# A chain of attention, routed experts and an FFT mixer: narrow experts reordered, one decode moved ahead

## The chip, the cores and the metric

The kernel runs on one core of one Trainium2 chip. The time is the device time of one execution in microseconds; the figure for a kernel is the median of its runs.

## What is computed

Three stages follow each other: attention with a local window and global keys, a stage of routed experts, and a mixer with a two-dimensional FFT. The change lies in the second:

```python
B, S, D, E, F = 2, 768, 512, 8, 1024
logits = x @ w_gate                     # one expert per token
local = sigmoid(x @ w_local)
for each sequence, for each token s:
    e = argmax(logits[s]) if s == 0 or local[s] < 0.5 else the expert of token s - 1
    out[s] = softmax(logits[s])[e] * (relu(x[s] @ w1[e]) @ w2[e])
```

The mixer behind it adds the real part of the FFT over tokens and features, normalises, and applies two dense layers (`w_ch1`, 512 x 2048, and `w_ch2`) with a residual. All data are float32.

## The kernel before

**Matrix products in two parts.** A float32 value is split in a high part that TensorE takes in one pass (`hi`) and the rest (`lo`). ScalarE (ACT) casts the high part, VectorE (DVE) subtracts it from the value. A product is then hi x hi, hi x lo and lo x hi: three matmuls for each step of the contraction. Weights, rows and hidden values all pass through this pair of steps.

**The ring of weights** (`Ring`). An expert has four pieces of 1 MB, kind `"e"`: two of w1, two of w2. A piece is loaded by SP into one of four raw buffers (`load`) and split into a slot (`take`: L1048 the cast on ACT, L1050 the subtract on DVE, in two halves of 1024 columns); when its last half is done, SP loads the piece that stands four places later into the buffer. The order of all pieces is the list `seq`. Between the experts' pieces stand eight of kind `"d"`: weights of the mixer that come as 64-bit words and are decoded to float32 ahead of time, so that the mixer can load them plain. A decode is one step on ACT (`start`, L1081), four on DVE (`bits`, L1090, L1092, L1094, L1096), all on a tile `dec` from a pool of two, and a DMA on POOL's queue that writes `dec` to `wmf` (L1014). `shade` says which decodes come with which expert's pieces: before, 2, 1, 1, 2, 1, 1 and 0 for experts 0 to 6.

**An expert** (`Moe.expert`). The tokens were sorted into lists by expert. A block is up to 128 tokens; POOL gathers its rows into a tile xg (`gathers`, L1133), PE turns them (`turn`, L1164), ACT and DVE split them into xh and xl (L1167, L1168). While expert e computes, the background `bg` prepares expert e + 1: its weights (`take`) and the turning of its rows (`tokens`). A call of `step` between matmuls lets the background issue one or more of its steps.

- *Wide* (two blocks): `first256` forms the hidden values of both, 256 columns wide (L1224), with relu by ACT and DVE (L1227, L1228); `third` adds a third block if there is one; `second` (L1204) multiplies by w2, block by block; `write` scales and scatters the result.
- *Narrow* (one block): `first128` forms h with tokens as rows (L1254), in two halves of 512. ACT copies each half out (`hs`, L1259), PE turns it (L1243), ACT and DVE form hh and hl (L1245, L1246). The second product starts when the first half's hh is there.

A branch at run time on the number of blocks chooses wide or narrow, on every engine. Expert 0 is always wide. In the runs here experts 1, 2, 3 and 5 are wide and experts 4 and 6 are narrow. Expert 7 is worked by sequence, two blocks with `first128`, and a third block with what is left of both; behind the turning of the third stands the check `rest(more)` for tokens beyond it, of which there are none here.

**The order ahead of expert 0** (`run`). The rows of expert 0 have to be gathered, after the list of tokens is written and its entries are loaded. Meanwhile PE multiplies constants (`keep_busy`, L50: 6, 6 and 3 matmuls of 512 columns), POOL and DVE clear the four xg tiles, and POOL issues two gathers and a scatter. The engines get to this place by a jump out of the attention's code.

**What sets the order.** Each engine works through its own instructions in the order in which this code issues them; the background decides between which matmuls a cast or a subtract comes to stand. DMA issues wait in the order of their queue: SP's for weights and entries, POOL's for gathers, scatters and the write to `wmf`.

## Time and profile before

| what | us |
|---|---|
| median of 3 runs (631.21 to 633.63) | 632.18 |
| the profiled execution, its own time | 635.4 |
| its span, first to last instruction | 633.6 |
| PE busy in the span | 609.5 |
| DVE busy | 383.8 |
| ACT busy | 275.3 |
| POOL busy | 100.5 |

The mean granted clock of PE is 0.992 of full speed. On PE the first matmul of expert 0 starts at 127.17 us. A row in order of time gives the start, the duration, engine, line, operation, what it writes and reads, how many like it are run together, and in brackets for how long the engine had been idle before and what ended that; "issue" there means that the profile names nothing. A releaser is inferred from the times of semaphores.

### The profile page before, as it was taken

What the parts mean: (1) busy time and instruction counts of PE and PEld (TensorE: products, weight loads), DVE (VectorE), ACT (ScalarE), POOL (GpSimd) and SP (SyncE); (2) the same over time, 40 slices, a digit from 0 to 9 for tenths busy, and PEclk for the clock granted to TensorE, in tenths of its full rate; (3) what the DMA queues carried; (4) which work ended last, traced back from release to release, by engine and by line L of the source; (5) the groups of instructions that cost most, each with busy time, mean ns of one, the idle gap of its engine ahead of it and who ended that gap; (6) DMA issues with size and microseconds to landing.
All of it is one profiled execution on the core that took longest, in us unless ns stands there. A gap on an engine that the chain in (4) does not pass through costs nothing.

```text
span 633.6 us, 9722 instructions
## 1 busy us (share of the span) xinstructions
PE 609.5 (96%) x3506; PEld 494.1 (78%) x3507; DVE 383.8 (61%) x898; ACT 275.3 (43%) x548; POOL 100.5 (16%) x147
## 2 busy tenths in 40 slices
PE   9999998799999969898999999999999999999997
PEld 4777875499899849687867887888888888888885
DVE  5778786279786968661389987997531221272112
ACT  5789883266475556552434533441121221131010
POOL 2146662315313312300100000000000000000000
PEclk9999999999999989989999999999999999999999
DMA  8568762279978989961260242551100100100001
GB/s 278 187 204 203 201 120 68 49 283 337 372 250 278 335 288 327 339 210 66 87 250 32 95 173 92 187 190 63 67 0 1 32 36 0 67 2 0 1 0 66
DMA packets 25192, 92.49 MB, mean 146 GB/s; under 512 B 7645, under 2 KB 8797, under 8 KB 17185
## 3 DMA queue, kind: packets, MB, share of 16 engines
q1 hardware_dynamic: 19664, 79.50, 37.6%
q0 software_dynamic: 4736, 10.56, 4.6%
q10 hardware_dynamic: 720, 1.55, 0.7%
q8 instruction: 36, 0.59, 0.4%
q14 instruction: 36, 0.29, 0.2%
HBM read 81.00 MB, written 14.84 MB: 151 GB/s over the span
## 4 chain that ended last, share of the span: by engine, by line
PE 52%; DVE 1%; ACT 0%; issue 0%; DVEq 0%; ACTq 0%
PE h L1742 21%; PE acc L1757 7%; PE acc L1756 7%; PE acc L1758 7%; PE y L1204 1%; PE acc L1576 1%; PE acc L1562 1%; PE more L1254 1%; PE h L1254 1%; PE more L1204 1%; PE f L1708 1%; PE f L1605 1%; PE h L50 1%; PE f L1627 0%; DVE u L1767 0%; PE acc L1565 0%
## 5 line engine op out<-in xcount | busy, mean ns | idle before, releaser
L1747 DVE SCALAR_TENSOR_TENSOR hl<-h,hh 128x512 fp32r<-128x512 f32 x48 | 33.1, 689 | 117.5 <-ACT hh L1746 117.5
L1746 ACT ACTIVATE hh<-h 128x512 fp32r<-128x512 f32 x48 | 28.8, 600 | 164.3 <-PE h L1742 164.3
L1050 DVE TENSOR_TENSOR wide<-raws,wide 128x1024 fp32r<-128x1024 f32 (+1 forms) x38 | 44.8, 1201 | 24.4 <-ACT wide L1048 24.4
L168 ACT ACTIVATE t<-t,nm 128x256 f32<-128x256 f32 (+1 forms) x96 | 46.0, 480 | 10.7 <-DVE nm L159 9.9
L1742 PE MATMUL h<-un0h,wide 128*128 128x512 f32 (+1 forms) x136 | 42.4, 378 | 0.1
L1048 ACT CAST wide<-raws 128x1024 fp32r<-128x1024 f32 (+2 forms) x42 | 40.6, 993 | 4.1 <-PE acc L1758 3.4
L159 DVE CUSTOM_DVE_ANT_0 t<-sp,bias 128x256 f32<-128x256 f32 (+1 forms) x96 | 32.8, 398 | 8.3 <-PE sp L150 4.4
L1757 PE MATMUL acc<-wide,hh 128*128 128x512 f32 x96 | 37.8, 393 | 0.0
L1756 PE MATMUL acc<-wide,hh 128*128 128x512 f32 x96 | 37.6, 392 | 0.0
L1758 PE MATMUL acc<-wide,hl 128*128 128x512 f32 x96 | 37.5, 390 | 0.0
L1133 POOL DMA_INDIRECT xg<-xs,ent x23 | 28.7, 1250 | 39.9 <-PE y L1204 17.4
L1742 PEld LDWEIGHTS h<-un0h,wide 128*128 128x128 f32 x136 | 25.0, 188 | 5.0 <-ACT un0h L1517 0.3
L178 PE MATMUL tp<-consts,t 128*128 128x128 f32 x176 | 26.1, 283 | 1.7 <-ACT p L184 1.7
L178 PEld LDWEIGHTS tp<-consts,t 128*128 128x128 f32 x176 | 18.9, 141 | 9.3 <-ACT p L184 4.9
L1742 PE MATMUL h<-un0l,wide 128*128 128x512 f32 (+1 forms) x68 | 25.6, 377 | 0.0
L192 PE MATMUL sm<-p,vs 128*64 128x128 f32 x352 | 24.5, 279 | 0.0
L184 ACT COPY p<-tp 128x512 f32<-128x512 f32 (+1 forms) x48 | 24.3, 537 | 0.3 <-PE tp L178 0.3
L1081 ACT ACTIVATE dec<-raws 128x1024 f32<-128x1024 f32 x18 | 20.6, 1143 | 4.8 <-issue 4.8
L1224 PE MATMUL h<-xh,wide 128*128 128x256 f32 x160 | 22.5, 279 | 0.0
L1096 DVE SCALAR_TENSOR_TENSOR dec<-raws,dec 128x1024 int32<-128x1024 int32 x18 | 22.0, 1225 | 0.6
L1094 DVE SCALAR_TENSOR_TENSOR dec<-raws,dec 128x1024 int32<-128x1024 int32 x18 | 22.0, 1222 | 0.4
L192 PEld LDWEIGHTS sm<-p,vs 128*64 128x64 f32 x352 | 18.7, 136 | 3.8 <-issue 3.8
(474 smaller groups left out, 1602.3 us busy)
## 6 DMA issues: line engine op xcount, KB each, us to landing
raws<-we SPq DMA_DIRECT2D x31, 1024.0 KB
raws<-wm SPq DMA_DIRECT2D x18, 1024.0 KB
raws<-wmf SPq DMA_DIRECT2D x7, 1024.0 KB
wmf<-dec POOLq DMA_DIRECT2D x8, 512.0 KB
xs<-xrow SPq DMA_DIRECT2D x12, 260.0 KB
vs<-v SPq DMA_DIRECT2D x6, 512.0 KB
raws<-kq SPq DMA_DIRECT2D x3, 1024.0 KB
u<-x SPq DMA_DIRECT2D x6, 512.0 KB
```

The lines of the kernel that those rows point to most:

```text
L159: V.tensor_tensor_reduce(out=u.t[:, x, :u.W], in0=u.sp[:, j, k, :u.W], in1=bias[:, 4 * u.g + x, u.b0:u.b0 + u.W], scale=-0.125, scalar=3.0 ...
L168: A.activation(u.t[:, x, :u.W], u.t[:, x, :u.W], AF.Exp, bias=u.nm[:, x:x + 1], scale=-1.0, accum_out=u.den[:, x])
L178: T.transpose(u.tp[k][:, j, c], u.t[:, 2 * k + j, c * P:(c + 1) * P], st.ident)
L192: T.matmul(turned[j * D:j * D + D, k], vs[:, ti % KS, u.h + 2 * k + j], u.p[:, 2 * k + j, c], start=c == 0, stop=c == len(tiles) - 1)
L1048: (first or nc.scalar.copy)(hi[:, cs], raw[:, cs])
L1050: (eng() if callable(eng) else eng or nc.vector).tensor_tensor(lo[:, cs], raw[:, cs], hi[:, cs].bitcast(F32), op=ALU.subtract)
L1742: nc.tensor.matmul(ps[:, c], a[:, k], x[:, k, c], start=n == 0, stop=n == 11)
L1746: nc.scalar.activation(hh, ps, AF.Relu)
L1747: nc.vector.scalar_tensor_tensor(hl, ps, 0.0, hh.bitcast(F32), op0=ALU.max, op1=ALU.subtract)
L1756: T.matmul(acc[c], hh[:, cs], h2, start=first, stop=False)
L1757: T.matmul(acc[c], hh[:, cs], l2, start=False, stop=False)
L1758: T.matmul(acc[c], hl[:, cs], h2, start=False, stop=last)
```

## The change

- Only experts 2, 4 and 6 (the third, fifth and seventh) branch on the number of blocks. Experts 1, 3 and 5 always go the wide way. The hint to PE on the next branch stands at experts 1, 3 and 5.
- The narrow way takes one background step at a time in place of two, first the two pieces of the next expert's w1, then those of w2, then decodes if any. Its `hs` lie in the third rows' tile and a `ys` tile, not in `dec`.
- The decodes are spread 2, 1, 2, 1, 0, 1 and 0 over experts 0 to 6, and one (`FIRST`) comes before expert 0: it is the fifth piece of the ring, and DVE makes its first step, by two shifts, in place of ACT's.
- POOL clears all four xg tiles. Of the fill-in matmuls ahead of expert 0 the middle six are cut in four parts of 128 columns each.
- In expert 7 the third block's rows are turned in the background of the first block, and the check `rest(more)` stands behind the third block's result.

```diff
--- before.py
+++ after.py
@@ -43,11 +43,13 @@
 L2, L3 = 2, 3
 
 
-def keep_busy(nc, st, ps, n):
+def keep_busy(nc, st, ps, n, parts=1):
 
     x = st.busy
-    for _ in range(n):
-        nc.tensor.matmul(ps, x[:, :1].to_broadcast([P, P]), x.unsqueeze(1).to_broadcast([P, 8, D]), start=True, stop=True)
+    w = 8 // parts
+    for k in range(n * parts):
+        o = k % parts * w * D
+        nc.tensor.matmul(ps[:, o:o + w * D] if parts > 1 else ps, x[:, :1].to_broadcast([P, P]), x.unsqueeze(1).to_broadcast([P, w, D]), start=True, stop=True)
 
 
 def load_kq(nc, st, io, i, pairs=((0, B * H // 2),)):
@@ -671,6 +673,8 @@
 SPLIT = 6
 WARM = 6, 6, 3
 TOKENS = 4
+FIRST = 1
+DECODED = 2, 1, 2, 1, 0, 1, 0
 CASTS = (5, 6, 7, 8)
 RESTS = (24, 25, 26, 27)
 AHEAD = dict(enumerate([0, 1, 2, 2, 2, 1, 1, 1, 4, 0, 0, 0, 0, 0, 1, 0, 0, 4, 1, 1, 1, 0, 0, 0, 2, 1, 1, 1], 4))
@@ -948,7 +952,7 @@
         self.behind, self.whole = [], 2
         self.seq = []
         self.plan = self.shade()
-        self.seq = [("e", g) for g in range(4)]
+        self.seq = [("e", g) for g in range(4)] + [("d", n) for n in range(FIRST)]
         for a, b in self.plan:
             self.seq += a + b
         for m in range(len(MIX)):
@@ -958,14 +962,14 @@
     @staticmethod
     def shade():
 
-        d = iter([("d", n) for n in range(2 * EARLY)])
+        d = iter([("d", n) for n in range(FIRST, 2 * EARLY)])
         plan = []
         for e in range(E - 1):
             g = 4 * e + 4
             a = [("e", g), ("e", g + 1)]
             b = [("e", g + 2), ("e", g + 3)]
 
-            for _ in range(-(-min(e + 1, E - 2) * 2 * EARLY // (E - 2)) + -min(e, E - 2) * 2 * EARLY // (E - 2)):
+            for _ in range(DECODED[e]):
                 (a if len(a) == 2 else b).append(next(d))
             plan.append((a, b))
         plan.append(([("t", 0), ("t", 1)], []))
@@ -1004,7 +1008,7 @@
         r = self.at[kind, n]
         raw = self.st.raw[r % PIECES]
         if kind == "d":
-            words, t = self.start(r)
+            words, t = self.start(r, nc.vector if n < FIRST else None)
             yield
             for k, _ in enumerate(self.bits(words, t)):
                 if k != 0:
@@ -1072,13 +1076,16 @@
         hi, lo, raw = self.quarter(n, k)
         self.tc.nc.vector.tensor_tensor(lo, raw, hi.bitcast(F32), op=ALU.subtract)
 
-    def start(self, r):
+    def start(self, r, by=None):
 
         if r in self.begun or r >= len(self.seq) or self.seq[r][0] not in ("m", "m2", "d") or (self.seq[r][0] != "d" and MIX[self.seq[r][1]][0] < EARLY):
             return self.begun.get(r)
         t = self.work.tile([P, PW // 2], F32, name="dec")
         words = self.st.raw[r % PIECES].bitcast(I32).rearrange("p (n two) -> p n two", two=2)
-        self.tc.nc.scalar.activation(t, words[:, :, 1].bitcast(F32), AF.Abs)
+        if by:
+            by.tensor_scalar(t.bitcast(I32), words[:, :, 1], 1, 1, op0=ALU.logical_shift_left, op1=ALU.logical_shift_right)
+        else:
+            self.tc.nc.scalar.activation(t, words[:, :, 1].bitcast(F32), AF.Abs)
         self.begun[r] = words, t
         return words, t
 
@@ -1126,7 +1133,7 @@
         self.ps_x = pool("ps_x", 2, space=PSUM)
         self.ps_more = pool("ps_more", 3, space=PSUM)
         self.ps_y = pool("ps_y", 1, space=PSUM)
-        for x in self.xg[:2]:
+        for x in self.xg:
             tc.nc.gpsimd.memset(x, 0.0)
 
     def gather(self, out, table, idx):
@@ -1288,12 +1295,13 @@
             self.weight(e, (2,))
 
             with tc.If(n > 2):
-                for _ in self.turn(2, 0, self.place(e, 2)):
-                    pass
+                if e < LAST:
+                    for _ in self.turn(2, 0, self.place(e, 2)):
+                        pass
+                late = self.first128(w1, *self.more, spare, spare)
+                result(2, self.more[1], spare, "more", lambda: None, late)
                 if e == LAST:
                     self.rest(more)
-                late = self.first128(w1, *self.more, spare, spare)
-                result(2, self.more[1], spare, "more", lambda: None, late)
 
         def pieces():
             for units in ring.plan[e]:
@@ -1323,26 +1331,33 @@
                     result(at + 1, own(hs, 1), spare, "more")
 
         def narrow():
-            first, then = pieces()
-            bg.add(chain(*first))
+            units = [u for part in ring.plan[e] for u in part]
+            for u in units:
+                if u[0] == "d":
+                    ring.begun.pop(ring.at[u], None)
+            takes = {u: ring.take(*u) for u in units}
+            d = [takes[u] for u in units if u[0] == "d"]
+            bg.add(chain(*(takes["e", 4 * e + 4 + k] for k in range(2))))
             h = own((self.hh[0], self.hl[0]), 0)
-            late = self.first128(w1, own((self.xh[e % 2], self.xl[e % 2]), 0), h, (self.ps_h, "h"), (self.ps_x, "xtp"), step)
+            late = self.first128(w1, own((self.xh[e % 2], self.xl[e % 2]), 0), h, (self.ps_h, "h"), (self.ps_x, "xtp"), bg.step,
+                                 [self.place(e, 2)[:, :DM], self.work.tile([P, DM], F32, name="ys", bufs=2)])
             bg.drain()
-            bg.add(chain(*then))
+            bg.add(chain(*(takes["e", 4 * e + 6 + k] for k in range(2)), *d))
             calls = iter(range(8))
 
             def behind():
                 if next(calls) == TOKENS:
                     bg.add(self.tokens(e + 1))
-                bg.step(2)
+                bg.step()
 
             result(0, h, (self.ps_y, "y"), "ys", behind, late)
 
         if e < LAST:
             if e + 2 < E:
                 self.entries(e + 2)
+            if e % 2 and e + 1 < LAST:
                 tc.mark_branch_hint_location(f"wide{e + 1}", hint=(ahead > 1), engines=[mybir.EngineType.PE])
-            if e == 0:
+            if e == 0 or e % 2:
                 wide()
                 return
             with tc.If(n > 1, label=f"wide{e}") as arm:
@@ -1351,6 +1366,7 @@
                 narrow()
             return
 
+        bg.add(self.turn(2, 0, self.place(e, 2)))
         for c in range(2):
             x, h = (own(s, c) for s in ((self.xh[e % 2], self.xl[e % 2]), (self.hh[0], self.hl[0])))
             late = self.first128(w1, x, h, (self.ps_h, "h"), (self.ps_x, "xtp"), step, [x[:, :DM] for x in self.xg[:2]])
@@ -1421,24 +1437,25 @@
         nc = tc.nc
         ring = st.ring
         self.entries(0, (1, 2))
-        for x in self.xg[2:]:
-            nc.vector.memset(x, 0.0)
         rows = self.gathers(0, (1, 2))
         self.entries(1)
         w = ring.load(2 * PIECES - 2)
         tc.add_manual_dep(w.ins, rows[1].ins.name, mybir.DependencyInfo(mybir.DependencyClass.Sync, mybir.DependencyReason.DATA),
                           reason="this load would hold the rows up")
         self.scatter(st.ye, st.ent0[:, 1:2])
+        for n in range(FIRST):
+            for _ in ring.take("d", n):
+                pass
         spare = self.ps_more.tile([P, DM], F32, name="more")
         keep_busy(nc, st, spare, WARM[0])
         counts = nc.values_load(st.nch[0:1, E + 1:E + 2], min_val=0, max_val=2 * 4 ** E - 1)
-        keep_busy(nc, st, spare, WARM[1])
+        keep_busy(nc, st, spare, WARM[1], 4)
         for _ in self.tokens(0):
             pass
         keep_busy(nc, st, spare, WARM[2])
         ring.load(2 * PIECES - 1, nc.scalar)
         for e in range(E):
-            self.expert(e, (counts >> 2 * e) & 3 if e < LAST else counts >> 2 * e, counts >> 2 * E, (counts >> 2 * (e + 1)) & 3 if e + 2 < E else None)
+            self.expert(e, (counts >> 2 * e) & 3 if e < LAST else counts >> 2 * e, counts >> 2 * E, (counts >> 2 * (e + 1)) & 3 if e % 2 and e + 1 < LAST else None)
 
 
 def post(tc, ctx, st):
```

**ACT, the narrow way.** `wide` and `sl5h` are slots of the ring, `raws` its raw buffers. ACT in expert 4's narrow code, from the end of expert 3. Before:

```order
L1348 UNCONDITIONAL_BRANCH
L1048 CAST wide<-raws 128x1024 x4
L1259 COPY dec<-h 128x512
L1081 ACTIVATE dec<-raws 128x1024
L1245 ACTIVATE hh_6327<-xtp 128x4x128
L1259 COPY dec<-h 128x512
L1048 CAST wide<-raws 128x1024
L1245 ACTIVATE hh_6327<-xtp 128x4x128
```

The change:

```order
L1363 UNCONDITIONAL_BRANCH
L1052 CAST wide<-raws 128x1024 x2
L1266 COPY xg_6353<-h 128x512
L1052 CAST wide<-raws 128x1024
L1252 ACTIVATE hh_6327<-xtp 128x4x128
L1052 CAST wide<-raws 128x1024
L1266 COPY ys<-h 128x512
L1052 CAST wide<-raws 128x1024
L1252 ACTIVATE hh_6327<-xtp 128x4x128
```

Two casts have moved from ahead of the first copy of h to behind it, one by one, and the decode is gone from between the copy and hh.

**PE, expert 7's third block.** The rows from the second half of the first block to the third. Before:

```order
L1254 MATMUL h<-wide,xl_6349 128x512 x2
L1254 MATMUL h<-sl5h,xl_6349 128x512 x2
L1290 REGISTER_ALU
L1290 COMPARE_AND_BRANCH
L1164 MATMUL more<-consts,xg_6354 128x128 x4
L1395 REGISTER_ALU
L1395 COMPARE_AND_BRANCH
```

The change, from the start of expert 7:

```order
L1363 UNCONDITIONAL_BRANCH
L1261 MATMUL h<-wide,xh_6346 128x512 x3
L1171 MATMUL more<-consts,xg_6354 128x128 x4
L1261 MATMUL h<-wide,xh_6346 128x512
L1261 MATMUL h<-sl5h,xh_6346 128x512
```

and at the end of the first block:

```order
L1261 MATMUL h<-wide,xl_6349 128x512 x2
L1261 MATMUL h<-sl5h,xl_6349 128x512 x2
L1297 REGISTER_ALU
L1297 COMPARE_AND_BRANCH
L1261 MATMUL more<-wide,xh_6347 128x512 x4
```

The four transposes of the third rows (`more<-consts,xg`) have moved ahead by a whole block, and the third block's matmuls follow its branch without the check between.

**DVE, the wait for the first rows.** From the jump out of the attention to the first rows. Before:

```order
L1913 UNCONDITIONAL_BRANCH
L1425 MEMSET xg_6353 128x520
L1425 MEMSET xg_6354 128x520
L1434 TENSOR_LOAD nch
L1168 TENSOR_TENSOR xl_6348<-xtp,xh_6345 128x4x128 x2
```

The change:

```order
L1930 UNCONDITIONAL_BRANCH
L1086 TENSOR_SCALAR dec<-raws 128x1024
L1097 TENSOR_SCALAR dec<-dec 128x1024
L1099 TENSOR_SCALAR dec<-dec 128x1024
L1101 SCALAR_TENSOR_TENSOR dec<-raws,dec 128x1024
L1103 SCALAR_TENSOR_TENSOR dec<-raws,dec 128x1024
L1451 TENSOR_LOAD nch
L1175 TENSOR_TENSOR xl_6348<-xtp,xh_6345 128x4x128 x2
```

Five steps of a decode stand where the two memsets stood, ahead of the load of the block counts and of the first rows' xl.

## Rows read from the trace of the kernel before

**Rows 1.** Windows: busy us of PE, PEld, DVE, ACT, POOL; PEclk, DMA share, GB/s.

```profile
200.00:220.00 20.00, 19.85 (x128) 17.76 (x127) 18.88 (x25) 12.91 (x16) 4.55 (x4) 1.00 0.77 267
220.00:240.00 20.00, 14.54 (x56) 11.15 (x55) 13.44 (x14) 11.55 (x15) 4.19 (x5) 0.83 0.82 292
260.00:280.00 20.00, 17.97 (x78) 14.36 (x78) 10.10 (x10) 10.61 (x14) 5.38 (x5) 0.91 0.78 274
```

**Rows 2.** What PE waited for, 126 to 325 us: total, times, longest.

```profile
PE y L1204 <- ACT hh L1245: 4.3, 1, 4.3
PE h L1254 <- ACT wide L1048: 2.0, 1, 2.0
PE more L1254 <- DVEq L1395: 1.6, 1, 1.6
```

**Rows 3.** PE in order of time, expert 4: start, us, instruction [idle before <-releaser].

```profile
220.58 1.09 PE L1254 MATMUL h<-wide,xh 128*128 128x512 f32 x4
...
226.10 0.66 PE L1243 MATMUL xtp<-consts,dec 128*128 128x128 f32 x4 [1.16 <-ACT dec L1259]
...
232.45 0.79 PE L1204 MATMUL y<-sl0h,hh 128*128 128x512 f32 x1 [4.30 <-ACT hh L1245]
...
242.30 1.10 PE L1224 MATMUL h<-xh,wide 128*128 128x256 f32 x8
```

**Rows 4.** PE in order of time, experts 6 and 7.

```profile
267.92 0.47 PE L1254 MATMUL h<-sl0h,xh 128*128 128x512 f32 x1 [2.03 <-ACT wide L1048]
...
275.56 1.32 PE L1204 MATMUL y<-wide,hh 128*128 128x512 f32 x5
...
282.44 1.10 PE L1254 MATMUL h<-wide,xh 128*128 128x512 f32 x4
...
288.47 0.60 PE L1164 MATMUL more<-consts,xg 128*128 128x128 f32 x4
290.67 1.16 PE L1254 MATMUL more<-wide,xh 128*128 128x512 f32 x4 [1.60 <-DVEq L1395]
```

**Rows 5.** ACT in order of time, expert 4.

```profile
221.66 3.90 ACT L1048 CAST wide<-raws 128x1024 fp32r<-128x1024 f32 x4
225.47 0.58 ACT L1259 COPY dec<-h 128x512 f32<-128x512 f32 x1
230.80 1.12 ACT L1081 ACTIVATE dec<-raws 128x1024 f32<-128x1024 f32 x1 [4.75 <-issue]
```

**Rows 6.** POOL in order of time, the write-out ahead of expert 4's decode.

```profile
221.12 0.59 POOL L1014 DMA_DIRECT2D wmf<-dec  x1 [0.68 <-DVE dec L1096]
```

**Rows 7.** DVE in order of time, expert 4's first subtracts.

```profile
222.80 4.63 DVE L1050 TENSOR_TENSOR wide<-raws,wide 128x1024 fp32r<-128x1024 f32 x4 [1.98 <-ACT wide L1048]
```

**Rows 8.** ACT in order of time, the end of expert 5.

```profile
257.33 2.02 ACT L1048 CAST wide<-raws 128x1024 fp32r<-128x1024 f32 x2
```

**Rows 9.** DVE in order of time, the wait for the first rows.

```profile
120.62 1.04 DVE L1425 MEMSET xg<- 128x520 f32 x2 [4.15 <-issue]
126.60 1.29 DVE L1168 TENSOR_TENSOR xl<-xtp,xh 128x512 fp32r<-128x512 f32 x2 [4.95 <-ACT xh L1167]
```

**Rows 10.** One decode's DVE steps: the window 231.9 to 236.4 us, tile dec alone.

```profile
231.90:236.40 4.50, 3.83 (x4) 0.50 0.45 189
```

**Rows 11.** PE in order of time, the wait for the first rows.

```profile
121.12 2.76 PE L50 MATMUL more<-busy 128*128 128x512 bf16 x12 [1.46 <-issue]
125.20 1.29 PE L1164 MATMUL xtp<-consts,xg 128*128 128x128 f32 x8 [1.31 <-issue]
```

**Rows 12.** POOL in order of time, three gathers.

```profile
121.55 1.02 POOL L1133 DMA_INDIRECT xg<-xs,ent  x1 [0.31 <-issue]
...
147.36 3.10 POOL L1133 DMA_INDIRECT xg<-xs,ent  x1 [3.39 <-PE more L1204]
...
215.44 1.33 POOL L1133 DMA_INDIRECT xg<-xs,ent  x1 [4.35 <-PE y L1204]
```

**Rows 13.** The page's part 2: GB/s in 40 equal slices of the span.

```profile
GB/s 278 187 204 203 201 120 68 49 283 337 372 250 278 335 288 327 339 210 66 87 250 32 95 173 92 187 190 63 67 0 1 32 36 0 67 2 0 1 0 66
```

## The prediction

> **What bounds the kernel now.** I read the profile in this order: windows of 20 us, the list of what TensorE (PE) waited for, then the rows in time order of each engine around the places that those two point to. In the windows the reader is to see that PE works nearly without a gap while wide experts run (19.85 of 20 us), and that two windows fall out: 220 to 240 us, where PE is busy 14.54 of 20 us at a granted clock of 0.83, and 260 to 280, with 17.97 at 0.91 [rows 1]. The waits from the first expert to the tail are few: 4.3 us for hh, 2.0 us at an h, 1.6 us at the third block [rows 2], and 1.16 us for a copy in expert 4 [rows 3]. The branches of the wide experts are not among them. So the time of this stage is PE's, and what can be won is those four waits and the slow clock behind two of them.
>
> **Expert 4** is narrow and lasts from 220.58 to 242.30, 21.72 us [rows 3]. What would it last if PE never waited, at full clock? The same work is seen undisturbed in two pieces: a first product with its four transposes from 282.44 to 288.47, 6.03 us, and a second with its twelve transposes from 275.56 to 282.44, 6.88 us [rows 4]. Together 12.91 us. The difference, 8.81 us, is what the present order costs, and two steps of ScalarE (ACT) make it. First, ACT has four casts ahead of the copy of h (3.90 us from 221.66), so the copy comes at 225.47 and PE's transposes wait 1.16 us [rows 3, 5]. Second, ACT's decode step (L1081) starts only at 230.80, after 4.75 us of idling, and the hh that PE needs stands behind it in ACT's order, so PE waits 4.30 us [rows 3, 5]. The row names no releaser. The step writes a `dec` tile; there are two of these, the narrow way holds its hs in one, and the other's former content was sent to `wmf` by a DMA issued only at 221.12 [rows 6]. So the step waits for that write to end, or for its raw piece. After the wait PE runs slow: 0.83 over 20 us is 6.8 us at the lower of its two clocks, 1.2 GHz. That is the rest of the 8.81 us.
>
> The change takes both away: two casts, not four, stand ahead of the copy, no decode is issued in expert 4 at all, and the hs lie in xg2 and ys. What is late next is VectorE (DVE). It has eight subtracts, 1.16 us each in a row of four, the first at 222.80 behind the first cast, 2.2 us after the expert's start [rows 7]; that takes it to 11.5 us. Two hl and two xl come on top; a pair of xl lasts 1.29 us [rows 9], so 2.6 us more, 14.1 us without any gap. Following the new order by hand, with the gaps where DVE waits for PE, I get the second xl at 14.9. PE has its 12.91 us, then eight matmuls of expert 5 that need only xh, 0.12 us apart, 0.93 us, and so wants that xl at 13.84: a new wait of 0.3 to 1.1 us. I take 1.1. Expert 4 gives 8.81 - 1.1 = **7.7 us**; bounds 6 (one more wait like the 1.6 us) and 8.5.
>
> **Expert 6** is narrow too. PE stops for 2.03 us ahead of its first matmul and then loses clock (0.91 of the window) [rows 1, 4]. From 267.92 to 282.44 are 14.52 us. The work alone is 12.91, so the slow clock costs 1.61 us, and the stop adds 2.03: 3.64 us lost. The wait names an ACT cast, but the last one that this matmul can mean ended at 259.35 [rows 8]. So it is none of the data, and I read it as PE's own instruction stream after the jump into the narrow code. Expert 4 is entered by the same jump, without a stop [rows 3]. What differs is where the code lies: counted in the program, a matmul as two instructions, the narrow code of expert 6 begins 2 instructions ahead of a multiple of 256, that of expert 4 begins 122 ahead. In the changed program the two begin 116 and 98 ahead. The bounds are 0 and 3.6; I take **3.6**, since both new places are like the one that did not stop.
>
> The Trainium skill (Runtime: NRT & Kernel Launch, "Instruction fetch mechanics") says that instructions come in blocks of 256, fetched in order, and that a taken branch out of the window forces a fetch. The stop agrees with it, though no row here tells a fetch from another stall. By that rule alone a taken jump over a whole wide way would stop wherever it lands; expert 6 would then gain nothing and the sum be 8.6 us.
>
> **Expert 7's third block.** PE turns it at 288.47 and then waits 1.60 us, behind the check for rows beyond the third block, which isn't taken, and the xl that DVE makes after it [rows 4]. In the changed order the turn stands behind the third matmul of the first block, some 5 us ahead of its use, and the check behind the third result. The transposes are only moved. **1.6 us**, bounds 1.0 and 1.6.
>
> **The wait for the first rows.** Here the change adds. DVE is idle from 121.66 to 126.60 [rows 9] and now gets a decode in place of two memsets. Four steps of a decode last 3.83 us [rows 10]; the first is new (two shifts on DVE in place of ACT's step), and I bound it by 0.7 us, a short step of those four, and 1.2 us, a long one. From 120.62 the decode ends at 125.1 to 125.7, ahead of the xl at 126.60, so DVE's own time costs nothing; without that cover its 4.5 to 5.1 us would stand ahead of the xl. POOL's two more memsets lie ahead of the list's entries, which its gathers wait for. The 24 short fill-in matmuls have the columns of the six that they replace: PE's twelve took 2.76 us from 121.12, and PE then idled 1.31 us to the transposes at 125.20 [rows 11], so they may grow by 1.3 us for nothing.
>
> What costs is the gathers. The second of this place took 1.02 us beside an idle DVE; beside DVE's subtracts and decodes a gather took 1.33 us, and once 3.10 us [rows 12]. For two gathers that bounds the cost at 0 and 4.2 us; I take **0.7**, twice the difference to the 1.33 us, because the 3.10 us is seen once.
>
> The SBUF — State Buffer page of the Trainium skill (section "SBUF: two separate sides") speaks against this part: POOL and a DVE step in a two-port mode lock each other out of a shared port, so that a gather whose descriptors POOL writes waits until DVE lets go. The 3.10 us agrees with that, the 1.33 us hardly. By it the rows would come later by the short steps of the decode, some 2 us in place of 0.7, and the sum be 10.9 us.
>
> **The rest.** Experts 1, 3 and 5 lose a branch at which PE did not wait: 0. Expert 2 now has two decodes, as expert 3 had; there DVE was busy 18.88 of 20 us and PE 19.85 [rows 1], so 0, and at worst one DVE step, 1.2 us.
>
> **The sum.** 7.7 + 3.6 + 1.6 - 0.7 = 12.2 us. The profiled execution took 635.4 us, 1.8 beyond its span and 3.2 above the median of 632.18 us. Less 12.2 it gives 623.2, and the median 620.0: I forecast **620.0 us**. A difference under 0.5%, 3.2 us, can't be told from no change here.
>
> **The rivals.**
> 1. *Expert 6 still stops at its entry, or expert 4 now does.* For: a stop without a releaser is seen, and I infer its cause from places alone. 12.2 - 3.6 = 8.6: 623.6 us. Chance 0.17.
> 2. *The first rows come late*, one or both gathers being of the 3.10 us kind: 2 to 4.2 us in place of 0.7, 621.3 to 623.5 us. For: DVE now works through the whole of the gathers. Against: 1.33 us is the commoner size. 0.10.
> 3. *Expert 4 finds a new wait*, for its last raw pieces or for DVE. If ACT's 4.75 us was a load and not the write, half of the gain may go: 624 us, with rival 1 some 627. Against: its pieces are asked for earlier, as no decode's words stand between them. 0.08.
> 4. *Slower: the transfers become the bound.* The ten slices from 127 to 285 us moved 283, 337, 372, 250, 278, 335, 288, 327, 339 and 210 GB/s [rows 13], on average 302, or 47.8 MB in 158 us. The changed kernel must move the same in 146 us, at 327 GB/s. Were the rate to fall, with more asked for at once, to the first slice's 283 GB/s, the stretch would last 169 us: 643 us. It turns into a loss below 302 GB/s and into one that can be told below 296. Against: one slice held 372 GB/s, and the windows show the DMA engines 0.77 to 0.82 busy [rows 1], so there is room. 0.04.
> 5. *It does not do what it says*: ACT or DVE come to the narrow experts so late that the new order changes nothing: 629 to 633 us. 0.04.
>
> **How the numbers follow.** The forecast has 0.57, the rivals 0.17, 0.10, 0.08, 0.04 and 0.04. The low end is all gains at their upper bound and no cost in the wait, 8.5 + 3.6 + 1.6 = 13.7, 618.5 us, less 1.5 for the scatter of the runs: 617.0. The high end takes in rivals 1 to 3, and 1 and 2 together: 626.0. Faster by over 0.5% is under 629.0 us: the forecast and rivals 1 to 3 hold 0.92, of which I take off 0.04 for costs that add up: 0.88. Within 0.5%: 0.07; slower: 0.05.
>
> **What would show it.** Right: expert 4 lasts 13.5 to 15 us, the ACT decode and PE's 4.3 us are gone, the clock stays at 1.00 from 220 to 240 us; expert 6 starts without a stop and lasts 13 us; no 1.6 us at the third block; expert 0's first matmul comes by 128.2 us. Wrong: PE at the lower clock anywhere from 127 to 290 us, a stop of 2 us at a narrow entry, or over 2 us of waiting for an xl or a raw piece.

## The result and the profile after

The changed kernel takes 625.47 us, median of 4 runs (624.24 to 627.69); the kernel before, beside it, 632.19 us (4 runs, 631.21 to 633.63). The ratio is 0.9896, 95% interval 0.986 to 0.9932: faster by 6.7 us. That lies in the forecast range, 0.5 us below its upper end, and is about half of the 12.2 us that were forecast. The profiled execution took 624.7 us, its span is 622.9 us.

Windows of the changed kernel, columns as in [rows 1], and one more, 280 to 300 us, in which expert 7 works:

```profile
200.00:220.00 20.00, 19.07 (x125) 17.08 (x124) 16.70 (x21) 12.66 (x16) 3.64 (x5) 1.00 0.88 292
220.00:240.00 20.00, 19.31 (x106) 16.01 (x106) 13.01 (x15) 13.88 (x18) 5.12 (x6) 1.00 0.92 328
260.00:280.00 20.00, 20.00 (x101) 16.41 (x100) 13.22 (x17) 14.74 (x20) 2.00 (x3) 1.00 0.83 290
280.00:300.00 20.00, 19.41 (x91) 15.61 (x90) 5.84 (x7) 7.61 (x11) 1.83 (x2) 1.00 0.01 4
```

PE is busy 19.31 us where it was 14.54, and 20.00 where it was 17.97, at a clock of 1.00. But from 200 to 220 us, where it had been busy 19.85, it now misses 0.93. What PE waits for, from 126 to 325 us, total, times and longest:

```profile
PE h L1231 <- DVE hl L1235: 0.8, 1, 0.8
PE h L1231 <- DVE pc L1187: 0.7, 1, 0.7
PE y L1211 <- PEq L1411: 0.6, 1, 0.6
```

The three waits of [rows 2], 7.9 us, and the 1.16 us for the copy [rows 3] are gone; three of 0.6 to 0.8 us have come, 2.1 us. PE in order of time, the starts of experts 4 to 7, the second product of expert 7's third block, and the block behind it:

```profile
222.33 1.09 PE L1261 MATMUL h<-wide,xh 128*128 128x512 f32 x4
...
226.53 0.60 PE L1250 MATMUL xtp<-consts,xg 128*128 128x128 f32 x4
...
228.38 0.40 PE L1211 MATMUL y<-sl0h,hh 128*128 128x512 f32 x1
...
235.39 1.20 PE L1231 MATMUL h<-xh,wide 128*128 128x256 f32 x8
237.29 0.73 PE L1231 MATMUL h<-xl,wide 128*128 128x256 f32 x4 [0.69 <-DVE pc L1187]
...
259.87 0.39 PE L1261 MATMUL h<-sl0h,xh 128*128 128x512 f32 x1
...
272.75 0.86 PE L1261 MATMUL h<-wide,xh 128*128 128x512 f32 x3
...
291.93 0.50 PE L1211 MATMUL y<-sl0h,hh 128*128 128x512 f32 x1 [0.59 <-PEq L1411]
...
297.99 1.09 PE L1261 MATMUL h<-wide,xh 128*128 128x512 f32 x4
```

Start to start, expert 4 lasts 13.06 us (before 21.72 [rows 3]), expert 5 24.48 (before, to the late start of expert 6, 25.62 [rows 3, 4]), expert 6 12.88 (14.52 [rows 4]), expert 7's first block and third 25.24 (26.22). ACT in expert 4, the answer to [rows 5]:

```profile
223.23 2.00 ACT L1052 CAST wide<-raws 128x1024 fp32r<-128x1024 f32 x2
225.33 0.59 ACT L1266 COPY xg<-h 128x512 f32<-128x512 f32 x1
225.81 1.05 ACT L1052 CAST wide<-raws 128x1024 fp32r<-128x1024 f32 x1
227.17 0.60 ACT L1252 ACTIVATE hh<-xtp 128x512 fp32r<-128x512 f32 x1 [0.31 <-PE xtp L1250]
```

PE's new wait, at expert 5, ends with DVE's second xl:

```profile
236.55 0.68 DVE L1175 TENSOR_TENSOR xl<-xtp,xh 128x512 fp32r<-128x512 f32 x1
```

It ends 14.90 us after expert 4's start; the releaser that the row of PE names (`pc`) is the copy just behind it.

The loss is in expert 3. SP's loads in expert 2, then ACT, DVE and PE at the start of expert 3:

```profile
187.38 4.73 SPq L990 DMA_DIRECT2D raws<-we  x2
194.11 0.33 SPq L994 DMA_DIRECT2D raws<-wm  x1
...
201.32 1.05 ACT L1052 CAST wide<-raws 128x1024 fp32r<-128x1024 f32 x1 [2.64 <-DMA raws<-wm]
...
202.41 1.23 DVE L1054 TENSOR_TENSOR wide<-raws,wide 128x1024 fp32r<-128x1024 f32 x1 [4.48 <-ACT wide L1052]
...
204.29 0.39 PE L1231 MATMUL h<-xh,sl0h 128*128 128x256 f32 x1 [0.78 <-DVE hl L1235]
```

ACT's first cast of expert 3 waits 2.64 us, and the releaser is the load of decode words (`raws<-wm`), which that cast doesn't read: its piece of w1 (`raws<-we`) was asked for 6.73 us earlier. DVE's subtract and hl come late behind it, and PE waits 0.78 us. Expert 3 lasts 24.58 us in place of 23.43.

The wait for the first rows, DVE, POOL and PE:

```profile
120.01 0.69 DVE L1086 TENSOR_SCALAR dec<-raws 128x1024 int32<-128x1024 int32 x1 [2.84 <-issue]
...
120.30 1.36 POOL L1140 DMA_INDIRECT xg<-xs,ent  x1 [2.33 <-DMA ent<-list]
121.96 1.10 POOL L1140 DMA_INDIRECT xg<-xs,ent  x1 [0.30 <-issue]
...
123.46 1.23 DVE L1103 SCALAR_TENSOR_TENSOR dec<-raws,dec 128x1024 int32<-128x1024 int32 x1
...
125.63 1.17 PE L1171 MATMUL xtp<-consts,xg 128*128 128x128 f32 x8 [1.47 <-issue]
...
127.64 0.39 PE L1231 MATMUL h<-xh,sl0h 128*128 128x256 f32 x1 [0.20 <-ACT xh L1174]
```

The decode ends at 124.69 us, ahead of the rows, so DVE's own time is covered. Expert 0 starts at 127.64 us, 0.47 later than before. The first gather of before, beside the second in [rows 12], was:

```profile
120.16 1.08 POOL L1133 DMA_INDIRECT xg<-xs,ent  x1 [3.40 <-DMA ent<-list]
```

In both kernels it waits for the list's entries to land.

Added up, the two profiles differ by 8.66 (expert 4) + 2.78 (5 and 6) + 0.98 (7) - 1.15 (3) - 0.13 (0) - 0.47 = 10.7 us, which is the difference of their own times, 635.4 and 624.7. The medians differ by only 6.7.

### The profile page after: what moved, and what is told of

It reads as the page before. It is cut to its first block, busy times and chain, and to the rows that moved or that the text cites. A ratio compares the mean times of both kernels' runs of the same rounds, so it can differ in the third digit from the quotient of the medians.

```text
span 622.9 us, 9677 instructions
## 1 busy us (share of the span) xinstructions
PE 606.4 (97%) x3524; PEld 493.0 (79%) x3525; DVE 383.2 (62%) x897; ACT 274.1 (44%) x547; POOL 100.6 (16%) x149
## 4 chain that ended last, share of the span: by engine, by line
PE 51%; DVE 1%; ACT 0%; issue 0%; DVEq 0%; ACTq 0%
PE h L1759 21%; PE acc L1774 7%; PE acc L1773 7%; PE acc L1775 7%; PE y L1211 1%; PE acc L1593 1%; PE acc L1579 1%; PE h L1261 1%; PE f L1725 1%; PE f L1622 1%; PE h L52 1%; PE f L1644 0%; DVE u L1784 0%; PE acc L1582 0%; PE f L1625 0%; PE acc L1644 0%
## 5 line engine op out<-in xcount | busy, mean ns | idle before, releaser
L1759 PE MATMUL h<-un1h,wide 128*128 128x512 f32 x64 | 21.3, 396 | 0.0
```

What stands on the lines that cost most here:

```text
L1759: nc.tensor.matmul(ps[:, c], a[:, k], x[:, k, c], start=n == 0, stop=n == 11)
```

## The experiments

Four questions were open. Why does expert 3 wait (a load that its order doesn't need, or two decodes in expert 2 as such)? Why did expert 6 stop at its entry (the place of its code, as predicted, or the branch of the expert before)? What was the wait in expert 4 (the write of the `dec` tile, or its raw piece)? And how much do the profiles vary from run to run? Each kernel is compared with the kernel before in the same session; edits are to the changed kernel where nothing else is said.

**How much a profile varies.** `before_look` and `after_look` are the two kernels again, no edit.

> The kernel before once more, unchanged, for a second profile. The two profiles differ by 10.7 us of span, the medians by 6.7 us, so 4 us of the difference must lie in what differs from one execution to the next. Theory A (the waits that the change removes vary by themselves, and the first profile of before caught long ones): this profile's span is 629 to 631 us, and the 3 to 4 us that it is shorter are found in expert 4 (18 to 20 us in place of 21.7) or at the start of expert 6 (a stop under 1 us in place of 2.03). Theory B (the stage is the same each time and the changed kernel's own profile was a lucky one): expert 4 again 21.5 to 21.9 us, expert 6 again 16.5 us, and the span within 1 us of 633.6.

> The changed kernel once more, unchanged. Theory A: expert 4 again 13.0 to 13.2 us and expert 6 12.9 us, expert 3 again about 24.6 us with an ACT cast that waits over 2 us for its raw piece, span 622.4 to 625.9 us. Theory B: expert 4 or 6 has a new wait of 1 to 3 us that the first profile lacks, span 624.5 to 626.

Measured: 633.19 us for the kernel before (ratio to itself 0.9998, 0.9974 to 1.0022) and 626.31 for the changed one (0.9877, 0.984 to 0.9914). PE in the second profile of the kernel before:

```profile
231.60 0.50 PE L1204 MATMUL y<-sl0h,hh 128*128 128x512 f32 x1 [2.81 <-ACT hh L1245]
...
266.95 0.47 PE L1254 MATMUL h<-sl0h,xh 128*128 128x512 f32 x1 [2.29 <-ACT wide L1048]
```

The wait for hh is 2.81 us where [rows 3] have 4.30, and expert 4 lasts 18.95 us in place of 21.72; the stop at expert 6 stays. So Theory A holds for expert 4 and not for expert 6. In the changed kernel ACT's wait at expert 3 was 3.48 us in the second profile, and expert 3 lasted 25.41, with experts 4 and 6 as in the first: Theory A again.

**The wait at expert 3.** `ring_order`: the narrow way issues all pieces in the ring's order. Of the three experts that branch, only expert 2's order changes by this (4 and 6 have no decode), and expert 2 goes the wide way here: no instruction that runs is another one, only what the join behind the two ways has to wait for.

```diff
-            d = [takes[u] for u in units if u[0] == "d"]
-            bg.add(chain(*(takes["e", 4 * e + 4 + k] for k in range(2))))
+            bg.add(chain(*(takes[u] for u in ring.plan[e][0])))
...
-            bg.add(chain(*(takes["e", 4 * e + 6 + k] for k in range(2)), *d))
+            bg.add(chain(*(takes[u] for u in ring.plan[e][1])))
```

> The changed kernel, but the narrow code issues its decodes in the ring's order, behind the piece that they follow in the list, in place of behind all pieces. Of the three experts with narrow code only expert 2 has decodes, and it goes the wide way, so no instruction of expert 2 that runs here changes its place. Theory J (the join): behind the two ways of expert 2, expert 3's first cast waits for the load that brings its raw piece; in the changed kernel that load is the third of the stretch on the wide way and the fifth on the narrow way, so at the join ACT waits for both, and the fifth of the wide way is the load of decode words, issued 7 us later. Then here expert 3 lasts 23.4 us again (24.6, 25.4 and 29.2 in the three profiles with the changed kernel's order), no ACT cast there waits over 1 us, and the time is 623 to 624.5 us. Rival T (the transfers: two decodes in expert 2 ask for too much): expert 3 still lasts 24.5 us or more, time 625.5 to 626.5 us.

Measured: 623.72 us (4 runs, 623.46 to 623.79), ratio 0.9857, 0.9836 to 0.9879. ACT at the start of expert 3:

```profile
197.65 0.69 ACT L1193 ACTIVATE more<-more,pc 128x512 f32<-128x512 f32 x1 [4.80 <-DVE dec L1103]
198.23 1.04 ACT L1052 CAST wide<-raws 128x1024 fp32r<-128x1024 f32 x1
```

The cast follows at once and expert 3 lasts 23.42 us. That shows the cause. The piece that the cast reads is the third load of the stretch on the wide way; in the changed narrow way, with the decodes behind, it is the fifth, counted on another semaphore. The cast behind the join waits for the third and the fifth load, and on the wide way the fifth is decode words. The trace of the changed kernel has both: the cast waits on the semaphores of the loads issued at 187.38 and 194.11 us, whose last landings are at 193.16 and 201.25, and starts at 201.32. The time alone, beside 625.47 and 626.31 us in other sessions, would not tell the two kernels apart: their ratios' intervals overlap.

`even_none` keeps the changed narrow way and gives expert 2 no decode:

```diff
-DECODED = 2, 1, 2, 1, 0, 1, 0
+DECODED = 2, 2, 0, 2, 0, 1, 0
```

> The changed kernel with the decodes moved out of the experts that branch, 2, 2, 0, 2, 0, 1 and 0 behind the one in the wait. Theory J: expert 2's two ways have the same order of loads, expert 3 lasts 23.4 us, time 623 to 624.5 us, unless expert 4's first casts come late behind expert 3's two decodes, which in the kernel before they did not. Rival T: the late raw piece only moves from expert 3 to expert 2 or 4, which then last 1 to 5 us longer.

Measured: 625.28 us (5 runs, 623.41 to 625.75), 0.9883, 0.9863 to 0.9902. Expert 3 lasts 23.43 us, the wait is gone too. The median is 1.6 us above `ring_order`'s and above the 624.5 that was expected; the profiled execution was the fastest of the five, 623.41 us, so it can't show why.

**The stop at a narrow entry.** `before_shift` is the kernel before with 59 fill-in matmuls in expert 5's narrow way, which isn't run: the code behind it moves by 120 instructions.

```diff
         def narrow():
+            if e == 5:
+                keep_busy(tc.nc, self.st, self.ps_more.tile([P, DM], F32, name="more"), 59)
             first, then = pieces()
```

> The kernel before, with 59 fill-in matmuls added to expert 5's narrow code, which does not run here: nothing that runs changes, but PE's code from there on lies 120 instructions further on. Counted with the fill-in matmuls' weight loads apart, expert 6's narrow code then begins 234 instructions ahead of a multiple of 256, before 98; expert 4's stays at 218. Theory P (the place of the code decides the stop at a narrow entry): the entries without a stop so far began 212 or more ahead, those with one 178, 98 and 56; so no stop at expert 6, and the time 2 to 3 us below the kernel before. Theory K (the jump decides: a taken branch right behind another jump, over the narrow code of the expert before): the stop of about 2 us stays, and the time within 1 us of the kernel before.

Measured: 634.12 us, 1.0017, 0.9991 to 1.0043, and the stop at the entry of expert 6:

```profile
266.37 0.47 PE L1254 MATMUL h<-sl0h,xh 128*128 128x512 f32 x1 [2.10 <-ACT wide L1048]
```

`ring_shift` is the opposite trial: `ring_order` with 57 such matmuls in expert 4's wide way, which isn't run either.

```diff
         def wide():
+            if e == 4:
+                keep_busy(tc.nc, self.st, self.ps_more.tile([P, DM], F32, name="more"), 57)
             bg.add(chain(*first))
```

> ring_order, with 57 fill-in matmuls added to expert 4's wide code, which does not run here: nothing that runs changes, but the narrow code of experts 4 and 6 begins 99 and 117 instructions ahead of a multiple of 256, where ring_order has 213 and 231. Theory P (place): stops of 1.5 to 2.3 us at both entries, the time 3 to 5 us above ring_order's 623.7 us. Theory K (jump): no stop, 623.7 us within 0.5.

Measured: 624.97 us (4 runs, 622.67 to 625.55), 0.986, 0.9818 to 0.9902, 0.8 us beyond what Theory K allowed; in the profile expert 0 lasts 24.44 us where `ring_order` has 23.22, and the reason was not looked for. Both entries, without a wait ahead of them:

```profile
222.77 1.09 PE L1261 MATMUL h<-wide,xh 128*128 128x512 f32 x4
...
260.34 0.39 PE L1261 MATMUL h<-sl0h,xh 128*128 128x512 f32 x1
```

The place in a block of 256 is not the cause. By a count of the program's instructions with each weight load as one of its own, expert 6's narrow code begins 98 ahead of a multiple of 256 in the kernel before, where PE stops, and expert 4's 99 ahead in `ring_shift`, where it doesn't. This count stands 96 off the prediction's (98 and 218 for its 2 and 122), and no trace gives an address; but by either count `before_shift` puts expert 6 within 16 instructions of the place of expert 4, where PE does not stop.

`ring_branches` is `ring_order` with the branches of experts 1, 3 and 5 put back, and the hint at every expert:

```diff
-            if e % 2 and e + 1 < LAST:
+            if e + 2 < E:
                 tc.mark_branch_hint_location(f"wide{e + 1}", hint=(ahead > 1), engines=[mybir.EngineType.PE])
-            if e == 0 or e % 2:
+            if e == 0:
...
-            self.expert(e, (counts >> 2 * e) & 3 if e < LAST else counts >> 2 * e, counts >> 2 * E, (counts >> 2 * (e + 1)) & 3 if e % 2 and e + 1 < LAST else None)
+            self.expert(e, (counts >> 2 * e) & 3 if e < LAST else counts >> 2 * e, counts >> 2 * E, (counts >> 2 * (e + 1)) & 3 if e + 2 < E else None)
```

> As ring_order, but experts 1, 3 and 5 branch again on their blocks, as before, with hints for each. By the prediction's term 0: the time of ring_order within 1 us and no wait at the starts of experts 2, 4 and 6. Rival (the branches matter by where PE's code lies): a stop of about 2 us at the entry of expert 4 or 6, time 2 to 4 us above.

Measured: 628.98 us (9 runs, 627.62 to 632.82), 0.9959, 0.9936 to 0.9981, 5.3 us above `ring_order` in the same session. PE at the two entries:

```profile
223.06 1.17 PE L1261 MATMUL h<-wide,xh 128*128 128x512 f32 x4 [1.46 <-ACT more L1193]
...
262.67 0.47 PE L1261 MATMUL h<-sl0h,xh 128*128 128x512 f32 x1 [1.84 <-issue]
```

So the branch of the expert just before brings the stop, and its removal is what the change gains there. The branch comes back together with the narrow code behind it and with hints at every expert; which of the three makes the stop is not told apart. In the profiles the two kernels differ by 3.8 us, of which 3.3 are idle time at the two entries; for the rest of the 5.3 us no cause is shown.

**The wait in expert 4.** `before_hs` is the kernel before with the narrow way's hs in the third rows' tile and a `ys` tile, as in the change, and nothing else:

```diff
-            late = self.first128(w1, own((self.xh[e % 2], self.xl[e % 2]), 0), h, (self.ps_h, "h"), (self.ps_x, "xtp"), step)
+            late = self.first128(w1, own((self.xh[e % 2], self.xl[e % 2]), 0), h, (self.ps_h, "h"), (self.ps_x, "xtp"), step,
+                                 [self.place(e, 2)[:, :DM], self.work.tile([P, DM], F32, name="ys", bufs=2)])
```

> The kernel before, with the narrow way's hs in the tiles that the change gives them, in place of a dec tile; order and decodes as before. Theory W (the decode in expert 4 waits until the write of the former content of its dec tile is done): the decode now finds a tile whose write was issued 10 us earlier, so PE's wait of 4.3 and 2.8 us for hh in the two profiles falls under 1 us, expert 4 lasts 15 to 16.5 us (21.7 and 19.0), the time is 3 us or more below the kernel before. Theory L (it waits for its raw piece): no change, PE waits 2.5 us or more.

Measured: 628.69 us (10 runs), 0.9942, 0.9916 to 0.9968. ACT in expert 4:

```profile
224.56 0.58 ACT L1259 COPY xg<-h 128x512 f32<-128x512 f32 x1
225.03 1.17 ACT L1081 ACTIVATE dec<-raws 128x1024 f32<-128x1024 f32 x1
226.10 0.59 ACT L1245 ACTIVATE hh<-xtp 128x512 fp32r<-128x512 f32 x1
```

The decode starts behind the copy, where [rows 5] have 4.75 us of waiting: its raw piece had long been there, and the wait was for the write of the `dec` tile. The landings in the trace of before say the same: the raw piece's last is at 224.94 us, that of the write issued at 221.12 [rows 6] at 230.72, and the decode starts at 230.80. In `before_look` and `before_shift` it starts 0.07 us after that landing too. Expert 4 lasts 15.88 us in `before_hs`, and 4.2 us come off the median by this edit alone.

`old_narrow` is the changed kernel with the narrow way of before (four casts ahead, hs in `dec`, two background steps at a time); the decodes stay where the change put them.

```diff
...
+            first, then = pieces()
+            bg.add(chain(*first))
...
-            late = self.first128(w1, own((self.xh[e % 2], self.xl[e % 2]), 0), h, (self.ps_h, "h"), (self.ps_x, "xtp"), bg.step,
-                                 [self.place(e, 2)[:, :DM], self.work.tile([P, DM], F32, name="ys", bufs=2)])
+            late = self.first128(w1, own((self.xh[e % 2], self.xl[e % 2]), 0), h, (self.ps_h, "h"), (self.ps_x, "xtp"), step)
...
-                bg.step()
+                bg.step(2)
```

> The changed kernel with the narrow way's old order alone: four casts ahead of the first copy of h, hs in dec tiles, two background steps at a time; the decodes stay where the change put them, so none falls into expert 4 or 6. Theory A1 (the decode behind the copy was what cost): only the wait for the copy comes back, 1.2 us on expert 4 and something like it on expert 6, expert 4 lasts 14 to 15.5 us, the time is 1 to 3 us above the changed kernel's 625.5. Theory A2 (the order of the casts was what cost): PE loses its clock again, expert 4 lasts 18 us or more, the time is 629 us or more.

Measured: 625.27 us (4 runs, 624.93 to 625.59), 0.9865, 0.9836 to 0.9894. Experts 4 and 6 last 14.07 and 14.01 us, by waits for the copy such as

```profile
226.44 0.66 PE L1250 MATMUL xtp<-consts,dec 128*128 128x128 f32 x4 [0.96 <-ACT dec L1266]
```

but its narrow way has the ring's order, and expert 3 lasts 23.43 us. So most of the gain in expert 4 is the decode that is no longer there; the new narrow way brings 1 us in each narrow expert, and its price at expert 3 ate it up. Expert 4 came as Theory A1 has it, the time did not rise by the 1 to 3 us.

**The first rows.** `ring_first_none` is `ring_order` without the decode ahead of expert 0; expert 0 gets it:

```diff
-FIRST = 1
-DECODED = 2, 1, 2, 1, 0, 1, 0
+FIRST = 0
+DECODED = 3, 1, 2, 1, 0, 1, 0
```

> As ring_order, and no decode in the wait for the first rows: it goes to expert 0, which then has three. By the prediction's term the first matmul of expert 0 comes 0.7 us earlier than in ring_order; expert 0 may pay for its third decode, by up to 1.2 us. So -0.7 to +0.5 us against ring_order. Rival (the gathers do not feel the DVE steps): the first matmul at the same time within 0.3 us, and the time 0 to 1.2 us above ring_order's.

Measured: 626.45 us (5 runs, 625.9 to 627.08), 0.9904, 0.9885 to 0.9922. Expert 0 starts at 127.04 us (`ring_order` 127.33), and the time is 2.7 us above `ring_order`'s, outside both expectations: a third decode in expert 0 is too many. ACT and PE, expert 0's end and expert 1:

```profile
150.29 1.16 ACT L1088 ACTIVATE dec<-raws 128x1024 f32<-128x1024 f32 x1 [4.83 <-DMA wmf<-dec]
...
158.34 0.74 PE L1231 MATMUL h<-xh,wide 128*128 128x256 f32 x4 [2.40 <-DVE hl L1235]
```

A decode waits 4.83 us for a `dec` tile's write again, expert 1 lasts 26.16 us. The early decode saves 2.7 us behind its place; the 0.3 us at its place are less than one kernel's two profiles differ there (127.64 and 128.94).

**Expert 7's third block.** `old_third` turns it in its old place, with the check between:

```diff
-                if e < LAST:
-                    for _ in self.turn(2, 0, self.place(e, 2)):
-                        pass
+                for _ in self.turn(2, 0, self.place(e, 2)):
+                    pass
+                if e == LAST:
+                    self.rest(more)
                 late = self.first128(w1, *self.more, spare, spare)
                 result(2, self.more[1], spare, "more", lambda: None, late)
-                if e == LAST:
-                    self.rest(more)
...
-        bg.add(self.turn(2, 0, self.place(e, 2)))
```

> The changed kernel with expert 7's third block turned where it was, and the check for further rows between the turn and its first matmul. By the prediction's term it loses 1.6 us; by the two profiles (a wait of 1.60 us before, a new one of 0.59 us at the check behind the third result) 1.0 us: 626.5 us. Rival (the check costs the same in either place): 625.5 us, no wait of over 0.7 us ahead of the third block.

Measured: 629.45 us (5 runs, 626.46 to 631.33), 0.9926, 0.9894 to 0.9959; expert 7 lasts 26.22 us, 0.98 more. The median is some 3 us above the 626.5 that was expected, and the edit can't be charged with that: in the profile, the slowest of the five executions, ACT's cast at expert 3 waited 4.65 us, PE 2.8, the clock fell to 0.83 in the window from 200 to 220 us, and expert 3 lasted 29.24 us, at a place that the edit doesn't touch. Whether the other four lost their time there too is not shown.

**A version that beats both.** `ring_tokens` is `ring_order` with the next expert's rows turned earlier in a narrow expert, against the 0.69 us at expert 5:

```diff
-TOKENS = 4
+TOKENS = 1
```

> ring_order, with the next expert's rows turned three calls earlier in the narrow way's second product (TOKENS 1 in place of 4), so that DVE makes its xl ahead of one or two of the subtracts. If DVE's order is what the 0.69 us wait at the start of expert 5 comes from, that wait goes and the time is 0.5 to 1 us below ring_order's: a ratio to the kernel before of 0.984 to 0.985. Rival (DVE is the limit of the narrow expert as a whole): the wait moves to expert 5's later work or to the second product, and the time stays at ring_order's ratio of 0.9857.

Measured: 622.52 us (5 runs, 621.1 to 623.39) beside 634.08, ratio 0.9818, 0.9785 to 0.9851, the lowest median of all, though its interval overlaps that of `ring_order` (0.9836 to 0.9879), taken in another session. PE at the start of expert 5:

```profile
232.89 1.10 PE L1231 MATMUL h<-xh,wide 128*128 128x256 f32 x8
233.82 0.63 PE L1231 MATMUL h<-xl,wide 128*128 128x256 f32 x4
```

The wait is gone; expert 4 lasts 12.89 us and expert 5 23.42, as long as any undisturbed wide expert.

## Why the prediction was right or wrong

- **Expert 4, 7.7 us.** Right in its mechanism: both steps of ACT, the write that held the decode (`before_hs`, and the landings), and the new wait, 0.69 of the 1.1 us; the second xl, worked out by hand for 14.9 us, ended at 14.90. From profile to profile 8.66 less 1.06 in expert 5, 7.6 us. Its size against the median was off: the kernel before's expert 4 lasted 21.72, 18.95 and 20.63 us in three profiles with the same narrow code (the third is `before_shift`), on average 20.43, so a usual execution gains 6.3.
- **Expert 6, 3.6 us.** The amount was right (experts 5 and 6 from 40.14 to 37.36 us; with expert 5's 1.06 us taken out, 3.8; with 40.14, 39.75 and 40.22 us in three profiles of before, 3.7), the reason wrong: "What differs is where the code lies" fell with `before_shift` and `ring_shift`. The step that failed is "Experts 1, 3 and 5 lose a branch at which PE did not wait: 0": PE didn't wait at those branches, but at the entries that follow them, and `ring_branches` is 5.3 us slower. So this amount came out by luck: the 3.6 us were taken because of the new places, and came because of the branches.
- **Expert 7's third block, 1.6 us.** It gave 0.98, the lower bound: the wait of 1.60 us is gone, and 0.59 us stands behind the moved check, for which the sum had no price.
- **The first rows, -0.7 us.** The size was near, the reason is not borne out. Expert 0 started at 127.17, 127.80, 126.53 and 126.18 us in four profiles of before and its variants, on average 126.9, and in the nine of the changed kernel and its variants with the early decode on average 127.8 (126.57 to 128.94): 0.9 us. The two gathers together took 2.10 us in each of the four and 2.5 on average in the nine (2.14 to 3.14), so they did grow, by 0.4 us; twice the difference to the 1.33 us would have been 0.6, not 0.7. But from the start of the first gather to the first matmul it is 7.0 us in both. What is later is that start, 119.9 us on average and 120.7, and in each of these profiles it comes 0.8 us after the landing of the list's entries, with and without a decode beside it. Why the entries land later, or whether they only scatter, is open. By the rule of the Trainium skill (SBUF — State Buffer, "SBUF: two separate sides") that was weighed there it would have been some 2 us; these gathers, 1.36 and 1.10 us beside five steps of a decode, don't show such a lock. The decode itself took 4.68 us, between the two bounds (the upper one adds up to 5.0, not 5.1) and under the cover that was named.
- **Expert 2, "so 0, and at worst one DVE step".** This is the main miss among the terms. It asked whether DVE has room in expert 2 and not what stands at its end. The changed order of the narrow way, which isn't even run there, makes ACT wait for a later load at the join, and expert 3 lasts 1.2, 2.0 and 5.8 us longer in the three profiles that have it (the third is `old_third`), on average 3.0.
- **The start of the sum.** "Less 12.2 it gives 623.2, and the median 620.0": the profile of before lay 3.2 us above its median, and part of that was the very wait that was then taken off in full. With usual sizes the sum is 6.3 (expert 4) + 3.7 (6) + 1.0 (7) - 0.9 (first rows) - 0.1 (0) - 3.0 (3) = 7.0, and 6.7 were measured. The 3.0 is the weakest of these: by the two profiles of the changed kernel itself it is 1.6, and the sum 8.4.
- **The rivals and the range.** None of the rivals came as described; against rival 4, the window from 220 to 240 us moved 328 GB/s. The upper end of 626.0 us was set for rivals 1 to 3. The median reached 625.47 without any of them, by the loss at expert 3 and the start of the sum, which no rival names. That it lies inside is in part luck.
- **The signs.** Of the signs of being wrong one came: a wait of over 2 us for the load of a raw piece, 2.64 and 3.48 us on ACT at expert 3. Expert 4 lasted 13.06 us, below the 13.5 to 15 that were to show it right, and in the second profile expert 0 began at 128.94 us, later than 128.2. The other signs came as forecast.

Open stays why expert 4 did not stop in the kernel before, where expert 3 had its branch too, while it stops in `ring_branches`; and what the hints do, as no run takes them away alone.

## What to carry to other kernels

Where two ways join, the first instructions behind them can wait for what either way left: keep the order of loads the same in both, even in the one that rarely runs. A wait that depends on when a write lands is not a constant: read it in several profiles before it becomes a term, and don't take it off a median when the profile itself lay above that median. A wait without a releaser, or with one long done, has no one cause: here ACT waited for a write's landing in expert 4, and PE's stop at expert 6 came with a fetch of code. Look for a landing at its end first, then for branches ahead of it and transfers of instructions beside it.

## What the runs showed of the hardware

**The stop at an entry comes with a fetch of code.** The trace lists transfers of instructions by queue. It names no engine and no content; those of q8, 0.02 MB each, I take for PE's, as they come at PE's entries. Transfers of queue q8 (packets, MB, share of 16 engines) in `before_shift`, in the windows 263.7 to 263.8 and 267.9 to 268.0 us:

```profile
q8 instruction: 1, 0.02, 68.9%
...
q8 instruction: 1, 0.02, 69.3%
```

Each took 1.1 us, 68.9% of 16 engines over 0.1 us. In `ring_shift`, from 260.2 to 260.3 us, the only one from 255 to 275 us:

```profile
q8 instruction: 1, 0.02, 58.9%
```

In the six stops seen (expert 6 in the kernel before, `before_look`, `before_shift`, `before_hs` and `ring_branches`, and expert 4 in the last) such a transfer starts 2.49 to 2.64 us ahead of the first matmul, while PE is still at its last ones, and the next starts 1.6 to 2.0 us behind it. At the 22 narrow entries without a stop a transfer starts within 1 us of the entry, delays nothing, and the next is over 8 us away. I read that one as the block behind the target, and the target as brought earlier; that isn't shown. The Trainium skill (Runtime: NRT & Kernel Launch, "Instruction fetch mechanics") says that a taken branch out of the fetched window waits for a fetch. The six stops agree with it; the 22 jumps without a stop go over the same wide way, and whether their target had been fetched before is not shown. Of 18 entries with no other branch between hint and jump none stopped, of ten with one six did. So a hint may be what spares the stop, and a branch behind it what undoes it; that is an inference, as the hint stands in every run.

**A write from POOL's queue lands late.** The profile's page of the changed kernel gives a median of 7.5 us from issue to landing for the writes of `dec`:

```profile
wmf<-dec POOLq DMA_DIRECT2D x8, 512.0 KB, 7.5
```

That is over the four of the eight whose landing it can tell, 3.31 us ahead of expert 0 and 7.01 to 7.96 later. The write that held expert 4 in the kernel before took 9.60 us. With two `dec` tiles this is what a decode waits for as soon as three uses follow each other closely: 4.75 us in expert 4 of the kernel before, where the copy of h was one of the three, and 4.83 us in `ring_first_none`.
